# An attention and highway kernel: the first quad loaded and squared in halves, and the whole order planned again

## The chip, the cores and the metric

The kernel runs on one core of a Trainium2 chip. The metric is the device time of one execution in microseconds. Thirteen runs of the kernel before have a median of 274.4 us and lie between 272.18 and 276.83 us.

The core has five engines that run their own instruction lists in order. TensorE (PE) multiplies matrices and transposes. VectorE (DVE), ScalarE (ACT) and GpSimd (POOL) work on tiles, and SyncE (SP) issues most of the transfers. [...]

## The reference

```python
# q, k, v: (8, 12, 448, 64) float32; tau = 0.1
q_n = q / (norm(q, axis=-1) + 1e-6)
k_n = k / (norm(k, axis=-1) + 1e-6)
scores = q_n @ k_n.T / tau
attn = softmax(scores, axis=-1)
x = (attn @ v)                  # heads side by side: (3584, 768)
H = relu(x @ w_h)
T = sigmoid(x @ w_t + b_t)      # w_h, w_t: (768, 768)
out = T * H + (1 - T) * x
```

Because q_n and k_n have unit length, the scores are bounded, and the kernel takes no maximum before the exponential.

## The kernel before

**Tiles.** A *quad* is four heads of one batch, so there are 24 quads, three for each of eight batches. The q part (t = 0) and the k part (t = 1) of a quad have each 4 x 448 rows of 64 elements. They are held as 128 partitions by 14 groups by 64 elements, in one `raw` tile in float32: two halves of 7 groups, 448 elements in each partition.

**Steps of a quad.**

- `load_qk` (L279) issues one transfer of 448 KB for q and one for k on SyncE. The k load of quad 0 is issued on ScalarE's queue instead (L288). `load_v` (L301) does the same for v.
- `squares` (L353) makes `sq`, in float16, on ScalarE (one operation of 896 elements), on VectorE, or on GpSimd (two of 448). VectorE sums each group of 64 into `n2` (L392), and for some quads GpSimd first adds the two half rows (`folds`, L409).
- `rsqrt_act` (L436) makes the inverse norm `rs` with two ScalarE operations, Ln and Exp, over q and k together. Later quads use Newton steps on VectorE in `rsqrt` (L451).
- `norms` (L512) multiplies `raw` by `rs` into `qn`, on VectorE (one operation for each of q and k) or on GpSimd (two). `qn` is then transposed into `qT`, either by seven TensorE transposes and a copy, or by a DMA transpose on SyncE.
- `cast_v` (L578) casts v to float16 into `vm`, on ScalarE or VectorE.
- `quad` (L603) computes seven sets of scores on TensorE (L624) into `sp` in PSUM, two buffers of it. ScalarE takes their exponential into `e` (L635), 896 elements an operation, 168 in all. TensorE multiplies `e` with `vm` into `u` (L675), and VectorE divides by the sum into `x` (L726). From quad 12 on, two sets of scores go out together.

**The feed-forward part.** `ffn` (L757) and `quarters` (L796) take 28 row tiles of `x`, transpose them to `xT`, and multiply them with the two weights in matmuls of 384 columns (L818). Tanh on ScalarE gives the gate. VectorE, or for some tiles GpSimd, combines the result (L836 to L911). The weights come by four transfers that GpSimd issues (`load_w`, L323). The first row tile can start only when the first batch's attention is done, so its work runs some quads behind the attention and alone at the end.

**What sets the order.** Each step is registered as an operation with an engine, an assumed duration, a due time and what it depends on. `Plan.run` (L55) then goes through all of them once, before the program is built. It keeps a clock for each engine, picks the ready operation with the smallest start plus a share of its due time, and so fixes the order in which every engine gets its instructions. On the chip these orders are fixed; only the waits move. Which engine does a step is written out in strings, one letter for each quad or row tile (L221 to L235): `SQ_E` for squares, `NORM` for norms, `TURN` for transposes and their copies, `VM` for the casts of v, `XT` for the transposes of x, `GATE` and `BIAS` for the feed-forward part.

For transfers the planner keeps one shared clock `dma_free`. It lets SyncE issue when that clock is at most 5 us ahead, and it takes a load as done 1.1 us after its data (L148). A matmul group whose tile shape differs from that of the one before it is charged 93 ns (`SWITCH`). The shapes are "quad" (scores), "row" (`u`) and "full" (the rest).

Of the kernel before, what the change touches and what calls it, by code (L numbers as in the profile page):

```python
# [8 lines left out]
FP32 = mybir.dt.float32  # L9
FP16 = mybir.dt.float16  # L10
# [10 lines left out]
class Plan:  # L21
# [7 lines left out]
    AHEAD = 15  # L29
    NEAR = 60  # L30
    LATE = 0.04

    def __init__(self):
        self.ops = []
# [20 lines left out]
    def run(self):  # L55
        for o in self.ops:
# [7 lines left out]
                    after.update((x.n, x) for x in d[1][:1] if x is not o)  # L64
            o.after = [x for n, x in after.items() if n not in deps]
            o.deps = list(deps.values())
        t_eng = {e: 0 for e in self.LAT}
        left = {o.n: len(o.deps) + len(o.after) for o in self.ops}
        outs = {o.n: [] for o in self.ops}
        for o in self.ops:  # L70
# [5 lines left out]
        while back:  # L76
            o = back.pop()
            due = 1e9 if o.pri is None else o.pri[0] if isinstance(o.pri, tuple) else o.pri
            for c in outs[o.n] if not isinstance(o.pri, tuple) else ():
                lat = o.dur + self.LAT[o.eng] + (o.size + 2000 if o.size else 0)  # L80
                due = min(due, c.pri - (self.SLACK * lat / 1000 if o in c.deps else 0))
            o.pri = due
            for d in o.deps + o.after:
                users[d.n] -= 1
                if not users[d.n]:
                    back.append(d)

        def arm(o):
            r = 0
# [16 lines left out]
        mode = ""  # L106
# [3 lines left out]
        while len(order) < len(self.ops):  # L110
            best = None
            for e, L in ready.items():
                if not L:
                    continue
                t = t_eng[e]
                pick = None
                for r, o in L:
                    s = max(t, r)
                    if e == "DVE" and o.kind == "lock":
                        s = max(s, port[0])  # L120
                    elif e == "POOL":
                        s = max(s, port[1])
                    elif e == "SP" and len(lanes) >= 8:
                        s = max(s, lanes[-8])
                    if e == "SP":
                        s = max(s, dma_free - 5000)
                    k = (max(s, t + self.NEAR) + (e != "SP") * self.LATE * 1000 * o.pri, o.pri, o.n)
                    if pick is None or k < pick[0]:
                        pick = (k, s, r, o)
                if best is None or pick[1] < best[1]:  # L130
                    best = pick
            _, s, r, o = best
            e = o.eng
            ready[e].remove((r, o))
            end = s + o.dur
            if e == "PE":
                if o.kind != mode:
                    end += self.SWITCH
                mode = o.kind
            elif e == "POOL":  # L140
                port[0] = end
            elif e == "DVE" and o.kind == "lock":
                port[1] = end
            t_eng[e] = end
            o.start, o.done = s, end
            if o.size:
                dma_free = max(dma_free, end + (-700 if o.kind == "turn" else 900)) + o.size
                o.done = dma_free + 1100  # L148
            if e == "SP":
                lanes.append(o.done)  # L150
            order.append(o)
            for c in outs[o.n]:
                left[c.n] -= 1
                if not left[c.n]:
                    arm(c)
# [7 lines left out]
def kernel(  # L163
# [18 lines left out]
    C = 7  # L182
# [35 lines left out]
    ones_row = const.tile([128, 128], FP16)  # L218
    eps = const.tile([128, 1], FP32)
    NV = 2  # L220
    SQ_E = ("APAAAAAAPAAAAAPAPAPAAAAP", "PPAPPPPPAAAAAAAAAAPPPAAA")  # L221
    FOLDS = "000000010102012120000110"
    NORM = ("DDDPPPPPPPPPPPPPPPPPDPPP", "DPPPPPPPPPPPPPPPPPPPPDPP")
    TURN = ("ADDDSSSSSSSSSSSSSSSSSSSS", "DDDDASSSSSSSSSSSSSSSSSSS")
    XT = "DDDDDDDDAAAAADSSASSSSSSSSSSS"
    ENG = {"A": "ACT", "D": "DVE", "P": "POOL"}
    PAIR = 12
    LEAD = 4
    GATE = "RRRRRRRRRDRRRRRPRRDRPPPRPRRD"
    BIAS = "MMMMMMMMMMMMMMMDDDMMDDDDDDDM"  # L230
    LATER = 3
    W_AT = 16
    RS = "AAAAAAADDDDDDDDDDDDDDDDD"
    SW_AT = 52
    VM = "UAAUAAUUDUUDDUDDUDDUUUUU"  # L235
    TAIL = 6
    vm_b = [const.tile([128, 6, C, 66], FP16, name=f"vm{i}") for i in range(NV)]
    e_b = [const.tile([128, 14 * S + 64], FP16, name=f"e{i}") for i in range(2)]
# [34 lines left out]

    o_fb = op("DVE", 700, -1, [], fill_b)


    raw_ops, sq_ops = {}, {}

    def load_qk(Q):  # L279
        b, qd = divmod(Q, NQ)  # L280
        ring, wait = P.buf("raw", N_RAW)
        st["ring_raw", Q] = ring
        got = []
        for t in range(2):
            def f(t=t):
                if t == 0:
                    st["raw", Q] = raw_p.tile([128, NG, D], FP32, name="raw")
                eng = nc.scalar if Q == 0 and t else nc.sync  # L288
                eng.dma_start(
                    st["raw", Q][:, NT * t : NT * t + NT].rearrange("x (h c) d -> x h (c d)", h=2),  # L290
                    (q, k)[t][b, 4 * qd : 4 * qd + 4]
                    .rearrange("n (p c) d -> (n p) (c d)", c=C)
                    .rearrange("(h x) f -> x h f", x=128),
                )
            o = op("SP", 60 if Q == 0 and t else 550, None, wait, f, kind="load", size=1200)
            wait = [("first", [o])] + wait if not got else wait
            got.append(o)
            ring.append(o)
        st["got", Q] = got

    def load_v(b):  # L301
# [51 lines left out]
    def squares(Q):  # L353
# [5 lines left out]
        for t in range(2):  # L359
# [4 lines left out]
            def f(t=t, eng=eng):  # L364
# [6 lines left out]
                else:  # L371
                    nc.gpsimd.tensor_mul(o[:, 0:C, :], i[:, 0:C, :], i[:, 0:C, :])  # L372

            def f2(t=t):
                o, i = st["sq", Q, t][:, C:NT, :], st["raw", Q][:, NT * t + C : NT * t + NT, :]
                nc.gpsimd.tensor_mul(o, i, i)  # L376

            a = op(eng, {"ACT": 840, "DVE": 1000, "POOL": 900}[eng], None,
                   wait + st["got", Q][t : t + 1], f, kind="lock" if eng == "DVE" else "")
            both = [a, a]  # L380
            if eng == "POOL":
                both[1] = op(eng, 900, None, [("first", [a])] + st["got", Q][t : t + 1], f2)
            ring += both
            st["ring_raw", Q] += both
            if not level:
# [46 lines left out]
        return [last]  # L432

    logs, switch = [], []

    def rsqrt_act(b, qd, reds):  # L436

        def f():
            n2, rs = nrm_tiles(b)
            nc.scalar.activation(rs[:, qd, :], n2[:, qd, :], AF.Ln, bias=eps[:, :])  # L440

        def g():
            rs = nrm_tiles(b)[1]
            nc.scalar.activation(rs[:, qd, :], rs[:, qd, :], AF.Exp, scale=-0.5)

        a = op("ACT", 200, None, reds + [o_fb, o_fe], f)
        z = op("ACT", 120, None, [a], g)
        logs.append(z)
        return z

    def rsqrt(b, qd, n, reds):  # L451
        due = None
# [52 lines left out]
        for it in range(2):  # L505
            for i in range(3 if eng == "DVE" else 4):
                last = op(eng, lens[0] if eng == "DVE" else lens[1], due, [last], newton(i, it),
                          kind="lock" if eng == "DVE" else "")
                ring_ta.append(last)
        return last  # L510

    def norms(Q, rs_op):  # L512
        b, qd = divmod(Q, NQ)
        for t in range(2):
            ring, wait = P.buf(f"qn{t}", N_QN)
            eng = ENG[NORM[t][Q]]

            parts = [(0, 2, 0, C)] if eng == "DVE" else [
                (h, h + 1, c0, c1) for h in range(2) for c0, c1 in ((0, C),)
            ]  # L520
            done = []
            for h0, h1, c0, c1 in parts:
                def f(t=t, eng=eng, h0=h0, h1=h1, c0=c0, c1=c1):
                    if h0 == 0 and c0 == 0:
                        st["qn", Q, t] = qn_p.tile([128, C, 128], FP16, name=f"qn{t}")
                    g = slice(NT * t, NT * t + NT)
                    rs = nrm_tiles(b)[1]
                    (nc.vector if eng == "DVE" else nc.gpsimd).tensor_mul(  # L528
                        st["qn", Q, t][:, :, :].rearrange("p c (h d) -> p h c d", h=2)[:, h0:h1, c0:c1, :],
                        st["raw", Q][:, g, :].rearrange("p (h c) d -> p h c d", h=2)[:, h0:h1, c0:c1, :],  # L530
                        rs[:, qd, g].rearrange("p (h c) -> p h c", h=2)[:, h0:h1, c0:c1]
                        .unsqueeze(3).to_broadcast([128, h1 - h0, c1 - c0, D]),
                    )

                n = (h1 - h0) * (c1 - c0) * D
                done.append(op(
                    eng, 1000 if eng == "DVE" else 145 + 1.68 * n, None,
                    ([("first", done[:1])] if done else wait) + [rs_op] + st["got", Q], f,
                    kind="lock" if eng == "DVE" else "",
                ))  # L540
            ring += done
            st["ring_raw", Q] += done
            st["ring_n", b] += done
# [2 lines left out]
            if TURN[t][Q] != "S":  # L546
                ringp, waitp = P.buf("pt", 2)

                def g(t=t):
                    st["tp", Q, t] = p_ps.tile([128, C, 128], FP16, name="tp", tag="pt")  # L550
                    for c in range(C):
                        nc.tensor.transpose(  # L552
                            st["tp", Q, t][:, c, :], st["qn", Q, t][:, c, :], ident[:, :]
                        )
# [3 lines left out]
                    copy = nc.scalar.copy if TURN[t][Q] == "A" else nc.vector.tensor_copy  # L558
                    copy(st["qT", Q, t][:, :, :], st["tp", Q, t][:, :, :])

                w = op("PE", 360, None, done + [o_id] + waitp, g, kind="full")
                z = op(ENG[TURN[t][Q]], 840 if TURN[t][Q] == "A" else 540, None, [w] + wait2, h)
                ringp += [w, z]
                ring += [w]
            else:
                def g(t=t):
                    st["qT", Q, t] = qt_p.tile([128, C, 128], FP16, name=f"qT{t}")
# [10 lines left out]
    def cast_v(b):  # L578
# [3 lines left out]
        for i in range(NQ):  # L582
            how = VM[NQ * b + i]
            got = []
            for h0, n in ((0, 1), (1, 1)) if how == "U" else ((0, 2),):
                def f(g=slice(2 * i + h0, 2 * i + h0 + n), how=how):
# [2 lines left out]
                        st["vr", b][:, g, :].rearrange("p i (c d) -> p i c d", c=C),  # L589
                    )  # L590
                got.append(op(
                    "ACT" if how == "A" else "DVE", {"A": 840, "D": 540, "U": 530}[how], None,
                    wait + [o_fv[b % NV], st["gotv", b][i]], f, kind="lock" if how == "D" else "",
                ))
            outs.append(got)
# [432 lines left out]
```

## Time and profile before

The page gives one profiled execution. Its own time was 274.4 us, and the span from its first to its last instruction is 272.6 us.

| Engine | busy us | share of the span | instructions |
|---|---|---|---|
| PE, matmuls | 240.3 | 88% | 4221 |
| PEld, weight loads beside them | 137.2 | 50% | 4221 |
| DVE | 226.1 | 83% | 496 |
| ACT | 207.7 | 76% | 284 |
| POOL | 154.7 | 57% | 170 |

| Group | count | mean ns | idle before it |
|---|---|---|---|
| ACT exponentials `e`<-`sp`, L635 | 168 | 922 | 19.7 us, of it 19.3 waiting for scores |
| PE feed-forward `pt`<-`w`,`xT`, L818 | 600 | 327 | 3.9 us |
| PE `u`<-`vm`,`e`, L675 | 2688 | 195 | 6.3 us |
| PE scores `sp`<-`qT`,`qT`, L624 | 672 | 377 | 3.8 us |
| POOL norms `qn`<-`raw`,`rs`, L528 | 84 | 970 | 42.5 us |
| ACT squares `sq`<-`raw`, L368 | 32 | 968 | 4.8 us, of it 4.5 waiting for loads of q |

A group's row gives the operation's duration and the idle time of its engine just before it, with what ended that idle time. The duration of a matmul includes its way through the array, so many overlap, and 600 x 327 ns are not 600 turns of the engine. An engine's share of the whole span hides that the kernel passes through stages: at the start little runs, in the middle attention and feed-forward overlap, and in the last 30 us only feed-forward is left. Windows of the trace show these stages apart.

### The profile page before, as it was taken

How to read it: one execution, taken by the hardware profiler on the slowest of the kernel's cores; microseconds unless marked ns; L12 is line 12 of the kernel's file. 1: busy time of each engine (PE TensorE's matmuls, PEld its weight loads, DVE VectorE, ACT ScalarE, POOL GpSimd, SP SyncE). 2: the span in 40 equal slices, each digit the busy share in tenths (PEclk: the TensorE clock that was granted, in tenths of full speed). 3: DMA queues.
4: the chain of work that ended last, by engine and by line, in shares of the span. 5: the costliest groups of instructions: out<-in, count | busy, mean ns of one | idle time of the engine just before them, and what ended most of it. 6: DMA issues, size and time to landing. Idle time of an engine off the chain costs nothing. (4 is left out here: it accounts for less than half of the span.)

```text
span 272.6 us, 9928 instructions
## 1 busy us (share of the span) xinstructions
PE 240.3 (88%) x4221; PEld 137.2 (50%) x4221; DVE 226.1 (83%) x496; ACT 207.7 (76%) x284; POOL 154.7 (57%) x170
## 2 busy tenths in 40 slices
PE   0277869989699999999999999999899999998991
PEld 0235546545345456555655556455456455565560
DVE  2998578499889989887999999899998786579793
ACT  3498799998979897899888898997677687821220
POOL 2869487975284993599419943976085004460500
PEclk9999798999999999999999999999999999999999
DMA  7999969998989999999999899999758535315323
GB/s 250 381 386 328 232 127 303 172 272 257 320 201 304 152 255 217 327 190 262 315 350 199 247 261 239 206 248 266 203 119 142 134 82 90 89 58 142 109 101 115
DMA packets 72061, 58.95 MB, mean 216 GB/s; under 512 B 48336, under 2 KB 68304, under 8 KB 72016
## 3 DMA queue, kind: packets, MB, share of 16 engines
q1 hardware_dynamic: 70144, 55.49, 79.7%
q0 software_dynamic: 1600, 2.36, 4.8%
q8 instruction: 33, 0.54, 0.8%
q10 hardware_dynamic: 272, 0.46, 0.5%
q14 instruction: 12, 0.10, 0.1%
HBM read 38.14 MB, written 11.01 MB: 180 GB/s over the span
## 5 line engine op out<-in xcount | busy, mean ns | idle before, releaser
L635 ACT ACTIVATE e<-sp 128x896 f16<-128x896 f32 x168 | 145.8, 922 | 19.7 <-PE sp L624 19.3
L818 PE MATMUL pt<-w,xT 128*128 128x384 f16 x600 | 116.2, 327 | 3.9 <-DVE o L911 1.7
L528 POOL TENSOR_TENSOR qn<-raw,rs 128x448 f16<-128x448 f32 x84 | 78.9, 970 | 42.5 <-DVE rs L494 36.3
L818 PEld LDWEIGHTS <-xT 128*128 128x128 f16 x672 | 59.2, 98 | 52.1 <-issue 16.1
L675 PE MATMUL u<-vm,e 64*128 64x65 f16 x2688 | 59.1, 195 | 6.3 <-DVE x L726 2.5
L675 PEld LDWEIGHTS <-e 64*128 64x128 f16 x2688 | 49.2, 97 | 30.3 <-issue 19.6
L624 PE MATMUL sp<-qT,qT 64*64 64x448 f16 x672 | 55.8, 377 | 3.8 <-ACT e L635 2.5
L392 DVE TENSOR_REDUCE n<-sq 128x7 f32<-128x448 f16 x60 | 34.3, 608 | 6.2 <-ACT sq L368 6.2
L889 DVE SCALAR_TENSOR_TENSOR pt<-tt,pt 128x384 f32<-128x384 f16 x56 | 31.3, 560 | 8.7 <-ACT tt L846 4.9
L368 ACT ACTIVATE sq<-raw 128x896 f16<-128x896 f32 x32 | 30.2, 968 | 4.8 <-DMA raw<-in_q_dram 4.5
L624 PEld LDWEIGHTS <-qT 64*64 64x64 f16 x672 | 15.6, 105 | 27.6 <-issue 22.5
L846 ACT ACTIVATE tt<-pt 128x384 f16<-128x384 f32 x44 | 21.9, 498 | 9.5 <-DVE pt L836 5.6
L726 DVE TENSOR_TENSOR x<-u,rd 128x384 f16<-128x384 f32 x48 | 24.5, 551 | 0.7
L904 DVE SCALAR_TENSOR_TENSOR pt<-pt,x 128x384 f32<-128x384 f32 x36 | 20.2, 561 | 5.7 <-PE pt L818 3.7
L419 POOL TENSOR_TENSOR fold<-sq 128x448 f32<-128x448 f16 x18 | 18.7, 1056 | 9.3 <-ACT sq L368 9.3
L372 POOL TENSOR_TENSOR sq<-raw 128x448 f16<-128x448 f32 x16 | 16.2, 1010 | 12.2 <-DMA raw<-in_k_dram 6.6
L846 ACT ACTIVATE tt<-sp 128x384 f16<-128x384 f32 x12 | 5.9, 490 | 21.1 <-DVE sp L836 19.2
L587 DVE CAST vm<-vr 128x448 f16<-128x448 f32 (+1 forms) x33 | 21.4, 669 | 0.1
L911 DVE SCALAR_TENSOR_TENSOR o<-x,pt 128x384 f32<-128x384 f16 x36 | 19.8, 550 | 0.7
L552 PE MATMUL tp<-ident,qn 128*128 128x128 f16 x63 | 6.7, 270 | 12.0 <-DVE qn L528 12.0
L857 POOL TENSOR_TENSOR g<-tt,x 128x384 f16<-128x384 f16 x8 | 7.3, 912 | 16.4 <-ACT tt L846 16.4
L376 POOL TENSOR_TENSOR sq<-raw 128x448 f16<-128x448 f32 x16 | 16.0, 1002 | 0.0
(53 smaller groups left out, 174.4 us busy)
## 6 DMA issues: line engine op xcount, KB each, us to landing
raw<-in_q_dram SPq DMA_DIRECT2D x24, 448.0 KB, 6.4
vr<-in_v_dram SPq DMA_DIRECT2D x24, 448.0 KB, 5.1
raw<-in_k_dram SPq DMA_DIRECT2D x23, 448.0 KB, 6.5
out_dram<-o SPq DMA_DIRECT2D x24, 384.0 KB, 3.5
out_dram<-o SPq DMA_DIRECT2D x8, 192.0 KB, 2.9
w<-in_moe_w_t_dram POOLq DMA_DIRECT2D x2, 576.0 KB, 11.7
w<-in_moe_w_h_dram POOLq DMA_DIRECT2D x2, 576.0 KB, 13.0
qT<-qn SPq DMA_TRANSPOSE x39, 4.1
```

What stands on the lines that cost most here:

```text
L368: nc.scalar.activation(o, i, AF.Square)
L392: nc.vector.reduce_sum(n2[:, qd, NT * t + g0 : NT * t + g0 + n], src()[:, g0 : g0 + n, 0:width], axis=AX.X,)
L528: (nc.vector if eng == "DVE" else nc.gpsimd).tensor_mul(st["qn", Q, t][:, :, :].rearrange("p c (h d) -> p h c d", h=2)[:, h0:h1, c0:c1, :] ...
L587: (nc.scalar.copy if how == "A" else nc.vector.tensor_copy)(vm[:, g, :, 0:D], st["vr", b][:, g, :].rearrange("p i (c d) -> p i c d", c=C),)
L624: nc.tensor.matmul(sp[64 * half : 64 * half + 64, h, 0:S].rearrange("x (c p) -> x c p", c=C), lhsT=kT[hp, ci, 64 * half : 64 * half + 64], ...
L635: nc.scalar.activation(e[:, o : o + 2 * S].rearrange("x (a p c) -> x a p c", a=2, c=C), st["sp", Q, ci][:, :, 0:S].rearrange("x a (c p) -> ...
L675: nc.tensor.matmul(u[:, s, slot * (D + 1) : (slot + 1) * (D + 1)], lhsT=e[sp, o : o + 128], rhs=vm[sp, 2 * qd + h, c, 0 : D + 1], start=(c ...
L726: nc.vector.tensor_mul(st["x", b][:, :, 4 * qd : 4 * qd + 4, :].rearrange("p t (h s) d -> p t h s d", s=2)[:, :, :, s, :], u[:, s, :, 0:D] ...
L818: nc.tensor.matmul(loc["pt", qi], lhsT=loc["xT"][:, cc, :] if cc < CC else ones_row[:, :], rhs=w_f[w_i][:, cc, ms] if cc < CC else bth[:, ms],
L846: nc.scalar.activation(loc["tt", mh][:, :], loc["pt", qi], AF.Tanh)
L889: nc.vector.scalar_tensor_tensor(out=h, in0=loc["tt", mh][:, :], scalar=1.0, in1=h, op0=ALU.add, op1=ALU.mult)
L904: nc.vector.scalar_tensor_tensor(out=h, in0=h, scalar=0.0, in1=xf()[:, ms], op0=ALU.max, op1=ALU.subtract)
```

## The change

Quad 0 is loaded in four transfers of 224 KB (q first half, q second half, k first half, k second half), all on SyncE. Both its squares are made on ScalarE, in halves that each wait for their own transfer. Its Ln and Exp are split into one pair for q and one for k, and the Exp writes into a PSUM tile `u`, from which the norms of quad 0 read. These norms run on VectorE in two pieces each (4 and 3 groups), and the transposes follow in pieces of 4 and 3.

The planner's rules are changed: loads are taken as done 1.7 us after their data and held until the transfer clock is at most 3 us ahead; all engines start at 0.7 us; and on TensorE an operation whose shape differs from the last one is charged 60 ns more in the choice. The letters that give steps to engines are other ones, and with them and the new rules the order of the whole kernel is another. Two hooks, `NUDGE` and `WARM`, are added and do nothing with the values given.

```diff
@@ class Plan
+    MODE = 60
+    QUEUE = 3000
...
-        t_eng = {e: 0 for e in self.LAT}
+        t_eng = {e: 700 for e in self.LAT}
...
-                        s = max(s, dma_free - 5000)
-                    k = (max(s, t + self.NEAR) + (e != "SP") * self.LATE * 1000 * o.pri, o.pri, o.n)
+                        s = max(s, dma_free - (self.QUEUE if o.kind == "load" else 5000))
+                    k = (max(s, t + self.NEAR) + (e != "SP") * self.LATE * 1000 * o.pri
+                         + (e == "PE" and o.kind != mode) * self.MODE, o.pri, o.n)
...
-                o.done = dma_free + 1100
+                o.done = dma_free + (1700 if o.kind == "load" else 1100)
@@ the letters
-    SQ_E = ("APAAAAAAPAAAAAPAPAPAAAAP", "PPAPPPPPAAAAAAAAAAPPPAAA")
-    FOLDS = "000000010102012120000110"
-    NORM = ("DDDPPPPPPPPPPPPPPPPPDPPP", "DPPPPPPPPPPPPPPPPPPPPDPP")
-    TURN = ("ADDDSSSSSSSSSSSSSSSSSSSS", "DDDDASSSSSSSSSSSSSSSSSSS")
-    XT = "DDDDDDDDAAAAADSSASSSSSSSSSSS"
+    SQ_E = ("AAAADPAAPAAAAAPAAPPAPPAP", "APPPPPPDAAAAAAAAAADAAAAA")
+    FOLDS = "000000002102012212101110"
+    NORM = ("DDDDDPPPPPPDDPPPPPPPPPDD", "DPPPPPPPPPPPPPPPPPPPPPPP")
+    TURN = ("DDDAADSSSDSSSSSSSSSSSSSS", "ADDDDSSDDSSSSSSSSSSSSSSS")
+    XT = "DDDADASDSSADDSSSSSASSSSSSSSS"
...
-    GATE = "RRRRRRRRRDRRRRRPRRDRPPPRPRRD"
-    BIAS = "MMMMMMMMMMMMMMMDDDMMDDDDDDDM"
+    GATE = "RRRRRRRRRRRRRRRPRRDRPPPRRRRD"
+    BIAS = "MMMMMMMMMMMMMDMDDDMMDDDDDDDM"
-    W_AT = 16
+    W_AT = 20
+    SPLIT = "100000000000000000000000"
-    SW_AT = 52
-    VM = "UAAUAAUUDUUDDUDDUDDUUUUU"
+    SW_AT = 40
+    VM = "DAAAAAUUAUDUUUDUUUAAAAAA"
@@ load_qk
-        for t in range(2):
+        for t, h, n in ((0, 0, 1), (0, 1, 1), (1, 0, 1), (1, 1, 1)) if Q == 0 else ((0, 0, 2), (1, 0, 2)):
...
-                eng = nc.scalar if Q == 0 and t else nc.sync
-                eng.dma_start(
+                hs = slice(2 * h, 2 * h + 2 * n)
+                nc.sync.dma_start(
@@ squares
+                a = op(eng, 460, None, wait + got[:1], lambda fq=fq: fq(0))
+                both = [a, op(eng, 460, None, [("first", [a])] + got[1:], lambda fq=fq: fq(1))]
@@ rsqrt_act, for each of the two parts of quad 0
+                nc.scalar.activation(rs[:, qd, gs], n2[:, qd, gs], AF.Ln, bias=eps[:, :])
...
+                    if part[0] == 0:
+                        st["rsp"] = u_ps.tile([128, 2, 512], FP32, name="u")
+                    o = st["rsp"][:, part[0], 0:NT]
+                nc.scalar.activation(o, rs[:, qd, gs], AF.Exp, scale=-0.5)
@@ norms
-            parts = [(0, 2, 0, C)] if eng == "DVE" else [
+            parts = [(0, 2, 0, C)] if eng == "DVE" and Q else [
+                (0, 2, 0, 4), (0, 2, 4, C)
+            ] if eng == "DVE" else [
...
+                    of = rs[:, qd, g] if Q else st["rsp"][:, t, 0:NT]
...
-                    ([("first", done[:1])] if done else wait) + [rs_op] + st["got", Q], f,
-                    kind="lock" if eng == "DVE" else "",
+                    ([("first", done[:1])] if done else wait) + [rs_op[t]] + st["got", Q][t], f,
+                    kind="lock" if eng == "DVE" and Q else "",
...
+                    ws = [op("PE", 220, None, done[:1] + [o_id] + waitp, lambda g=g: g(range(4)), kind="full")]
+                    ws.append(op("PE", 160, None, done[1:] + [("first", ws[:1])], lambda g=g: g(range(4, C)), kind="full"))
```

## The prediction

> **What bounds the kernel now.** I first read the windows of 10 us (columns: the stretch and its length; busy us and count on PE, PEld, DVE, ACT, POOL; granted clock; DMA share; GB/s).
>
> ```profile
> 30.00:40.00 10.00, 7.03 (x176) 4.89 (x177) 5.26 (x13) 9.11 (x15) 6.99 (x8) 0.84 0.91 166
> 60.00:70.00 10.00, 8.48 (x184) 4.60 (x183) 9.53 (x25) 8.72 (x11) 5.09 (x6) 1.00 0.91 277
> 110.00:120.00 10.00, 10.00 (x198) 5.46 (x198) 8.54 (x20) 9.20 (x12) 7.69 (x9) 1.00 1.07 288
> 160.00:170.00 10.00, 10.00 (x231) 5.91 (x230) 9.44 (x26) 9.18 (x13) 2.73 (x3) 1.00 1.03 252
> 210.00:220.00 10.00, 10.00 (x178) 5.30 (x172) 7.91 (x17) 7.59 (x11) 0.00 (x0) 1.00 0.59 151
> ```
>
> See that up to about 75 us ScalarE is the fullest engine while TensorE has gaps; later TensorE has none, with VectorE and ScalarE near 90% behind it. The chain of waits agrees: from 202 to 240 us it names only TensorE.
>
> ```profile
> 209.38 0.50 PE sp L624 x8
> 209.88 0.55 PE u L675 x28
> 210.43 1.73 PE pt L818 x10
> ```
>
> Busy time is not price on this engine, since a matmul's row holds its latency (326 ns mean at L818). So I read start to start in TensorE's timeline.
>
> ```profile
> 99.59 0.66 PE L818 MATMUL pt<-w,xT 128*128 128x384 f16 x3
> 100.18 0.38 PE L624 MATMUL sp<-qT,qT 64*64 64x448 f16 x4
> 100.49 1.15 PE L818 MATMUL pt<-w,xT 128*128 128x384 f16 x6
> 101.48 0.33 PE L818 MATMUL pt<-bth,ones_row 128*128 128x384 f16 x1
> 101.73 0.57 PE L624 MATMUL sp<-qT,qT 64*64 64x448 f16 x8
> 102.24 0.51 PE L774 MATMUL xp<-ident,xtail 128*128 128x128 f16 x6
> ```
>
> Three pt take 0.59 us and seven take 1.24, so one costs 0.163 and the group 0.10 on top. Four sp take 0.31 and eight 0.51: 0.05 each, 0.11 on top. Groups of u (28 in 0.55, 56 in 0.99) give 0.0157 each and 0.11. **Every change of tile shape costs TensorE about 0.11 us**, and the order of before has 280 of them: 31 us of a saturated engine.
>
> Last, the head, in the timeline of all engines.
>
> ```profile
> 5.20 0.95 ACT L368 ACTIVATE sq<-raw 128x896 f16<-128x896 f32 x1 [3.18 <-DMA raw<-in_q_dram]
> 5.54 0.93 POOL L372 TENSOR_TENSOR sq<-raw 128x448 f16<-128x448 f32 x1 [4.23 <-DMA raw<-in_k_dram]
> 8.41 0.32 ACT L440 ACTIVATE rs<-n,eps 128x28 f32<-128x28 f32 x1 [2.26 <-DVE n L392]
> 9.02 2.83 DVE L528 TENSOR_TENSOR qn<-raw,rs 128x896 f16<-128x896 f32 x2
> 12.87 0.62 DVE L559 COPY qT<-tp 128x896 f16<-128x896 f16 x1 [0.50 <-PE tp L552]
> 13.55 0.96 PE L624 MATMUL sp<-qT,qT 64*64 64x448 f16 x8 [0.72 <-DVE qT L559]
> 14.19 1.73 ACT L635 ACTIVATE e<-sp 128x896 f16<-128x896 f32 x2 [1.29 <-PE sp L624]
> ```
>
> Nothing covers this chain: load, square, sum, norm, transpose, copy. ScalarE's 168 exponentials start only at 14.19.
>
> **The head.** Four half loads leave on SyncE at 0.49 us each (its row of before), so the last is issued near 2.2 us instead of 0.77 on ScalarE's queue. [...] If the 1.5 us of extra issue were all paid, the last half would land at 5.54 + 1.5 = 7.0. The slice row shows 381 GB/s here, so a half of 224 KB takes 0.59 us, longer than its issue: the halves follow one another behind the same data. I take the row: the first lands about 3.6 us, the last about 5.3. ScalarE then squares four halves. [...] In the trace exponentials of 896 follow every 0.868 us and tanh of 384 every 0.38: 0.96 ns an element and almost nothing fixed, so a half costs 0.44 and splitting 0.06. [...] Last square done at 5.9, its sum at 6.5. GpSimd's 1.8 us for k (5.54 to 7.36) leaves the chain. Ln and Exp are split too, q's running during k's sums. The four norm pieces have 512 or 384 elements: the nearest row, x<-u,rd from PSUM, has 384 in 0.47 us start to start, so 0.6 + 0.47, twice: 2.1 against 2.83, since the pair of before ran into a GpSimd square (1.69 for the second, 1.14 for the first; that square took 1.80). Norms end at 8.7, transposes at 9.1, ScalarE's copy (0.89) at 10.1, first exponential 10.8: **3.4 us earlier**. The bounds are 0 (the next quad decides) and 3.9. Quad 1 keeps GpSimd squares and its k load arrives no earlier, but its Ln waited behind exponentials and sums (15.80), not on the load; I pass on 3.2.
>
> **TensorE by order.** Counted in the two built programs' instruction orders, which hold no time: changes of shape go from 280 to 235, minus 45 x 0.11 = -4.9 us. Transposes of qn go from 63 to 98, those of x from 90 to 72: +17 x 0.057 (six in 0.34) = +1.0. Two bias matmuls fewer: -0.3. Net -4.2. By groups of four quads (112 matmul sets of scores): 0, +2.7, -2.5, -2.9, -0.2, 0, and -1.1 after the last scores; the +2.7 is feed-forward and transposes moved earlier.
>
> **ScalarE.** Casts of v 4 to 12: +8 x 0.83; one qT copy more +0.8, one xT copy fewer -0.7, one square fewer -0.85, one Ln more +0.2: +6.1 us. In orders: quads 4 to 7 get +2.8 (37.3 to 40.1 us of ScalarE work in a stretch that lasted 39.5: it sticks out, I charge +1.0); quads 16 to 19 +2.2 (33.5 in 38.5, hidden under TensorE); quads 20 to 23 +2.8 (35.5 in a stretch of 35.5; charged +1.0, nothing if the casts fall in ScalarE's waits for scores, the full 2.8 if not). Stretch lengths come from the exponentials' busy time in the windows, 0.868 us each. These casts were hidden before on VectorE.
>
> **VectorE** sheds 12 casts (-8.4), 12 sums of 448 but gains 6 of folds (-4), gains four full norms (+6), four qT copies less two xT (+1.4), 2 us of feed-forward operations, and three squares that the trace of before lacks. Nearest is the norm of 896, 1.09 to 1.89 us by GpSimd's interference; I take 1.3, +3.9 in all, 3.3 to 5.7 at the ends. Together about +1, but moved forward: +6 in quads 0 to 3, where it had 7 us idle between 30 and 50 us; -2 to -4 in quads 8 to 11 and 16 to 23. GpSimd loses about 6 us and is at 57%: nothing. Gates: one late feed-forward tile leaves GpSimd's pair (0.92 + 0.91), on the chain at 253.12 to 255.03, for VectorE: up to -0.7, inside the tail's -1.1.
>
> **Queues.** Five qT transposes leave SyncE, three xT come. Loads are held until 3 us of data is queued rather than 5, and count as done 0.6 us later. Trace: loads took 6.4 us to land and, after the head, no wait on raw is large; later issue could cost a load's wait of 1 us or gain as much on transposes behind it; I take 0.
>
> **Sum.** Head -3.2; quads 4 to 7 +1.0; quads 8 to 11 limited next by VectorE's 34.8, so -1.3 of 2.5; quads 12 to 15 -2.7; 16 to 19 -0.2; 20 to 23 +1.0; tail -1.1: -6.5. Each engine is then above 90% in order, and waits grow; before, a stretch lasted 0.5 to 2.5 us above its largest sum. I keep -5.0. The span of 272.6 becomes 267.6. The profiled execution's time was 274.4, 1.8 more, and equals the median of the runs: **269.4 us**, chance 0.47.
>
> **Rivals.** (a) *Everything lands:* the stages give up -6.5 and the two charges are hidden: 274.4 - 8 = 266.4. For: ScalarE has 28.8 us idle between first and last exponential. Against: three engines near their sums. 0.14.
> (b) *The weights come late.* Their start time goes from 16 to 20 us, the last issue behind quad 3's norm near 31 instead of 25.9; they took 10.8 to 13.1 us to land, so 44. Feed-forward starts half a quad earlier in order: 45.8 - 3.2 - 2 = 40.6. TensorE would stand 3 us in a stretch where ScalarE waits behind it: 272.5. Against: VectorE and ScalarE may delay its start anyway. 0.13.
> (c) *Hidden:* the next quads' loads or VectorE (9.5 of 10 busy at 10 to 20 us) take the head, TensorE's saved switches turn into waits: 273.8. 0.12.
> (d) *ScalarE becomes the bound, and it is slower.* Place: exponentials from quad 4 on. If the 28.8 us of waits stay, because paired scores still come late in larger groups (two score buffers), the added 6.1 us are paid in full, and larger groups (my estimate) add 0.5 us of such waits in each of four stretches: 274.4 - 3.2 + 6.1 + 2.0 - 1.1 for the tail = 278.2. It decides once ScalarE's waits on scores stay above 17 us (19.3 now). Against: those waits were TensorE's own fullness, which falls. 0.14.
>
> **Numbers.** 0.5% is 1.4 us, about what this kernel's runs can tell from nothing. Faster (below 273.0): all of the forecast and (a), 0.08 of (b), 0.03 of (c): 0.72. Same: the rest of (b) and (c), with 0.01 of (d): 0.15. Slower: 0.13. The range of 266.0 to 275.0 leaves out most of (d) and a low edge of (a).
>
> **What would show it.** Right: first exponential near 10.8; 235 shape changes at the same 0.11; last exponential's end near 234 instead of 239.5; the tail after it about 1 us shorter; no TensorE gap at the first pt. Wrong: a wait of the first pt on w; ScalarE above 95% in quads 4 to 7 or waits on scores above 20 us; a wait of VectorE or ScalarE on raw past 20 us; score groups after which TensorE idles.

## The result and the profile after

The changed kernel takes 267.88 us (median of 11 runs, 267.30 to 269.53). The kernel before, run beside it, takes 274.25 (48 runs, 271.34 to 276.83). The ratio is 0.981, with a 95% interval from 0.977 to 0.984: about 6 us faster, with 269.4 forecast and 266.0 to 275.0 as the range. The profiled execution of after took 268.86 us, 1 us above the median, and its span is 267.1 where before's was 272.6. Ratios, here and below, leave out runs that were disturbed, and so can differ a little from the quotient of two medians. (The diff above misprints the new `XT`. It is "DDDADASADSSADDSSSSSASSSSSSSS", and the counts of the prediction were made with that.)

These are the same five windows of after as were read of before, in the same columns (stretch, length, busy us and count on PE, PEld, DVE, ACT and POOL, granted clock, DMA share, GB/s).

```profile
30.00:40.00 10.00, 7.47 (x182) 5.22 (x175) 7.05 (x14) 9.97 (x16) 8.66 (x9) 0.83 1.12 266
60.00:70.00 10.00, 9.77 (x228) 5.93 (x228) 9.47 (x27) 9.85 (x14) 6.68 (x8) 1.00 1.04 260
110.00:120.00 10.00, 10.00 (x216) 5.74 (x209) 9.08 (x20) 9.38 (x13) 9.92 (x11) 1.00 0.90 184
160.00:170.00 10.00, 10.00 (x206) 5.58 (x202) 9.51 (x27) 9.26 (x12) 2.94 (x4) 1.00 1.08 280
210.00:220.00 10.00, 10.00 (x223) 5.93 (x219) 5.73 (x13) 8.51 (x12) 0.07 (x1) 1.00 0.80 130
```

ScalarE is full at 60 to 70 us (9.85 of 10, before 8.72), and TensorE's gaps there have gone (9.77, before 8.48). At 210 to 220 VectorE is down from 7.91 to 5.73: the late casts of v have left it. The groups of exponentials and scores in after, and the scores in before:

```profile
L703 ACT ACTIVATE e<-sp 128x896 f16<-128x896 f32 x168 | 145.5, 925 | 11.1 <-PE sp L692 10.6
L692 PE MATMUL sp<-qT,qT 64*64 64x448 f16 x672 | 53.9, 376 | 8.1 <-ACT e L703 7.0
L624 PE MATMUL sp<-qT,qT 64*64 64x448 f16 x672 | 55.8, 377 | 3.8 <-ACT e L635 2.5
```

ScalarE waits 10.6 us for scores, where it waited 19.3, and TensorE now waits 7.0 us for ScalarE to empty a score buffer, where it waited 2.5. The time saved on TensorE has turned in part into waits on the next engine.

The price of a change of tile shape is read again in TensorE's timeline of after.

```profile
230.11 2.11 PE L886 MATMUL pt<-w,xT 128*128 128x384 f16 x12
232.15 0.57 PE L692 MATMUL sp<-qT,qT 64*64 64x448 f16 x8
232.65 0.84 PE L743 MATMUL u<-vm,e 64*128 64x65 f16 x42
233.42 0.66 PE L886 MATMUL pt<-w,xT 128*128 128x384 f16 x3
```

Start to start, 12 pt take 2.04 us (12 x 0.163 + 0.10 = 2.06), 8 sp take 0.50 and 42 u take 0.77 (42 x 0.0157 + 0.11 = 0.77). The prices of before hold in after.

Then the head, in the timeline of all engines.

```profile
0.74 0.87 SPq L312 DMA_DIRECT2D raw<-in_q_dram  x2
1.66 0.91 SPq L312 DMA_DIRECT2D raw<-in_k_dram  x2
3.31 1.23 ACT L405 ACTIVATE sq<-raw 128x448 f16<-128x448 f32 x2 [1.29 <-DMA raw<-in_q_dram]
5.70 0.58 ACT L405 ACTIVATE sq<-raw 128x448 f16<-128x448 f32 x1 [1.17 <-DMA raw<-in_k_dram]
7.43 0.58 ACT L405 ACTIVATE sq<-raw 128x448 f16<-128x448 f32 x1 [1.16 <-DMA raw<-in_k_dram]
9.57 1.61 DVE L588 TENSOR_TENSOR qn<-raw,u 128x384 f16<-128x384 f32 x3 [0.32 <-ACT u L497]
13.44 1.71 ACT L703 ACTIVATE e<-sp 128x896 f16<-128x896 f32 x2
```

The q halves are squared early, but ScalarE stands idle before each k half, and the last one can be squared only at 7.43. The first exponential comes at 13.44, which is 0.75 us earlier than before and not 3.4. What the DMA engines moved from 3 to 5 us, while these loads were in flight, is the last figure (GB/s) of these windows of before, after and e4. The last is a kernel described below, which loads the first quad whole again.

```profile
3.00:5.00 2.00, 0.00 (x0) 0.00 (x0) 0.00 (x0) 0.00 (x0) 0.00 (x0) 1.00 1.05 381
3.00:5.00 2.00, 0.00 (x0) 0.00 (x0) 1.05 (x2) 1.15 (x2) 0.00 (x0) 1.00 0.88 266
3.00:5.00 2.00, 0.00 (x0) 0.00 (x0) 0.00 (x0) 0.00 (x0) 0.00 (x0) 1.00 1.04 393
```

At the start of the feed-forward part TensorE's timeline shows the wait that rival (b) named.

```profile
44.55 0.65 PE L886 MATMUL pt<-w,xT 128*128 128x384 f16 x3
47.13 0.65 PE L886 MATMUL pt<-w,xT 128*128 128x384 f16 x3 [1.93 <-DMA w<-in_moe_w_h_dram]
47.70 0.57 PE L692 MATMUL sp<-qT,qT 64*64 64x448 f16 x8
```

How the difference builds up is read from the first exponential of each quad, after against before. The stages are differences of these; "quads 20 to 23" ends with the last exponential, and the last row is what follows it.

| stage | forecast us | measured us | standing at its end |
|---|---|---|---|
| head | -3.2 | -0.75 | -0.75 |
| quads 0 to 3 | 0 | -1.22 | -1.97 |
| quads 4 to 7 | +1.0 | -1.12 | -3.09 |
| quads 8 to 11 | -1.3 | -0.50 | -3.59 |
| quads 12 to 15 | -2.7 | +0.20 | -3.39 |
| quads 16 to 19 | -0.2 | -1.52 | -4.91 |
| quads 20 to 23 | +1.0 | -0.32 | -5.23 |
| after the last exponential | -1.1 | -0.27 | -5.5 |

The sums agree, -6.5 with -5.0 kept and -5.5 measured. The stages don't. So the experiments ask which parts of the change pay.

Each column of times is from one execution, and some of the experiments show how far that carries. e7, e10 and e12 below have the same instruction order as after on every engine up to 176 us. Their heads measure -0.53 to -1.18, and quads 8 to 11 -0.87 to -1.23; the other stages up to quad 15 agree with the table within 0.1. e6 has the order of before up to 188 us and yet stands 1.4 to 1.5 us later from quad 7 to quad 18. So a single stage is good to about 1 us, and quads 4 to 7 may have gained more than 1.12.

### The profile page after: what moved, and what is told of

Same layout as the page of the kernel before. It is cut to its first block, busy times and chain, and to the rows that moved or that the text cites. A ratio compares the mean times of both kernels' runs of the same rounds, so it can differ in the third digit from the quotient of the medians.

```text
span 267.1 us, 9962 instructions
## 1 busy us (share of the span) xinstructions
PE 236.1 (88%) x4236; PEld 136.4 (51%) x4236; DVE 223.8 (84%) x493; ACT 213.3 (80%) x295; POOL 148.2 (56%) x164
## 4 chain that ended last, share of the span: by engine, by line
PE 54%; DVE 21%; DMA 11%; ACT 7%; issue 3%; SPq 1%; DVEq 0%; ACTq 0%
PE pt L886 26%; PE u L743 12%; PE sp L692 11%; DMA w<-in_moe_w_h_dram 6%; ACT e L703 5%; DVE pt L957 4%; DVE pt L972 3%; DVE o L979 3%; DMA vr<-in_v_dram 3%; DVE n L432 2%; DVE x L794 2%; DMA raw<-in_k_dram 2%; PE sp L886 2%; PE xp L842 2%; PE tp L616 2%
## 5 line engine op out<-in xcount | busy, mean ns | idle before, releaser
L703 ACT ACTIVATE e<-sp 128x896 f16<-128x896 f32 x168 | 145.5, 925 | 11.1 <-PE sp L692 10.6
L588 POOL TENSOR_TENSOR qn<-raw,rs 128x448 f16<-128x448 f32 x76 | 74.0, 1004 | 39.1 <-DVE rs L551 19.4
L743 PE MATMUL u<-vm,e 64*128 64x65 f16 x2688 | 54.5, 192 | 0.6 <-issue 0.6
L459 POOL TENSOR_TENSOR fold<-sq 128x448 f32<-128x448 f16 x24 | 24.7, 1039 | 14.9 <-ACT sq L395 13.5
L432 DVE TENSOR_REDUCE n<-sq 128x7 f32<-128x448 f16 x48 | 27.7, 608 | 5.0 <-ACT sq L405 4.1
L395 ACT ACTIVATE sq<-raw 128x896 f16<-128x896 f32 x29 | 27.7, 965 | 0.0
L616 PE MATMUL tp<-ident,qn 128*128 128x128 f16 x98 | 9.9, 258 | 10.4 <-DVE qn L588 9.6
L399 POOL TENSOR_TENSOR sq<-raw 128x448 f16<-128x448 f32 x14 | 13.1, 934 | 10.8 <-DMA raw<-in_k_dram 8.9
L886 PE MATMUL sp<-w,xT 128*128 128x384 f16 x72 | 13.7, 326 | 1.7 <-DMA xT<-x 1.7
L616 PEld LDWEIGHTS <-qn 128*128 128x128 f16 x98 | 7.3, 116 | 13.5 <-DVE qn L588 10.6
L776 DVE RECIPROCAL rd<-u 128x12 f32<-128x12 f32 (+1 forms) x48 | 9.7, 202 | 5.0 <-PE u L743 4.5
```

Of the source, the lines that this page charges most:

```text
L395: nc.scalar.activation(o, i, AF.Square)
L432: nc.vector.reduce_sum(n2[:, qd, NT * t + g0 : NT * t + g0 + n], src()[:, g0 : g0 + n, 0:width], axis=AX.X,)
L588: (nc.vector if eng == "DVE" else nc.gpsimd).tensor_mul(st["qn", Q, t][:, :, :].rearrange("p c (h d) -> p h c d", h=2)[:, h0:h1, c0:c1, :] ...
L703: nc.scalar.activation(e[:, o : o + 2 * S].rearrange("x (a p c) -> x a p c", a=2, c=C), st["sp", Q, ci][:, :, 0:S].rearrange("x a (c p) -> ...
L743: nc.tensor.matmul(u[:, s, slot * (D + 1) : (slot + 1) * (D + 1)], lhsT=e[sp, o : o + 128], rhs=vm[sp, 2 * qd + h, c, 0 : D + 1], start=(c ...
L886: nc.tensor.matmul(loc["pt", qi], lhsT=loc["xT"][:, cc, :] if cc < CC else ones_row[:, :], rhs=w_f[w_i][:, cc, ms] if cc < CC else bth[:, ms],
```

## The experiments

Medians of kernels that ran together stand beside the same runs of before: 274.25 for e1 to e4, 274.15 for e5 to e8, 273.99 for e9 to e12. Times inside a kernel come from one profiled execution of it.

**e1: the head alone.** The kernel before with `load_qk`, `squares`, `rsqrt_act` and `norms` of after; rules and letters stay, but for the square of k in quad 0. (The planner's assumed durations of squares, norms and casts are those of after in e1 and e8.)

```diff
-    SQ_E = ("APAAAAAAPAAAAAPAPAPAAAAP", "PPAPPPPPAAAAAAAAAAPPPAAA")
+    SQ_E = ("APAAAAAAPAAAAAPAPAPAAAAP", "APAPPPPPAAAAAAAAAAPPPAAA")
```

> The kernel before with the new head alone (half loads, half squares, inverse norms in PSUM; old planner rules, old letters but ScalarE for the k squares of quad 0); 278 changes of tile shape on TensorE against 280. If the head carries the gain as sized in the prediction (3.2 us): 271. If it carries only what the trace of the changed kernel shows at the first exponential (0.75 us): 273.5. If what matters is the number of shape changes or the letters: 273.5 to 274.5, since neither moves.

Measured 274.91, ratio 0.9995 [0.995, 1.004]. The first exponential started at 12.47 us, 1.7 earlier, and the last one ended at 235.75, 3.8 earlier; the tail behind it grew from 33.06 to 34.85 us in the profile. That execution was the fastest of e1's twelve (272.40), and by their median the runs gained nothing. The head alone, with this order of the tail, is worth no time that can be measured.

**e2: the grouping of shapes alone.**

```diff
-                    k = (max(s, t + self.NEAR) + (e != "SP") * self.LATE * 1000 * o.pri, o.pri, o.n)
+                    k = (max(s, t + self.NEAR) + (e != "SP") * self.LATE * 1000 * o.pri
+                         + (e == "PE" and o.kind != mode) * 60, o.pri, o.n)
```

> The kernel before with one thing more in the planner's choice: 60 ns against a change of tile shape on TensorE. 239 changes against 280, all letters and the head as before. If shape changes are the price of the middle (0.11 us each, some 35 of the 41 in the stretch where TensorE has no gap): about 270.3. If the letters or the head carry the gain: 274 within 1.

Measured 274.19, ratio 1.0005 [0.997, 1.004], with 239 changes of shape instead of 280. By quad 13 the exponentials were 4.97 us ahead of before. At quad 23 1.70 was left, and the tail was 1.6 us longer.

**e3: after without the grouping.**

```diff
-    MODE = 60
+    MODE = 0
```

> The changed kernel with that 60 ns set to 0: 265 changes against 235. Shape changes: 267.9 + 30 x 0.11 = 271.2, somewhat less where TensorE has gaps. Letters or head: 268 within 1.

Measured 272.62, ratio 0.998 [0.994, 1.002], with 265 changes of shape: 4.7 us above after. The same rule that brought nothing in e2 is worth most of the gain here.

**e4: after with the first quad loaded whole,** k on ScalarE's queue as before; squares, norms and all else as in after.

```diff
-        for t, h, n in ((0, 0, 1), (0, 1, 1), (1, 0, 1), (1, 1, 1)) if Q == 0 else ((0, 0, 2), (1, 0, 2)):
+        for t, h, n in ((0, 0, 2), (1, 0, 2)):
...
-                nc.sync.dma_start(
+                (nc.scalar if Q == 0 and t else nc.sync).dma_start(
```

> The changed kernel with quad 0 loaded as before: two whole transfers, k issued on ScalarE's queue; squares still in halves, inverse norms still in PSUM; 238 shape changes against 235. If half loads gain what the prediction gave them: first exponential 2 us or more later and 270 or above. If the loads are bound by the data and not by how they are cut: first exponential within 0.7 us of 13.44 either way, and 267.3 to 268.6. If halves on one queue cost (the last k half landed at 7.4 us, the whole k of before at 5.5): first exponential earlier, 12 to 13, and up to 1 us faster.

Measured 267.00 (266.43 to 267.86), ratio 0.976 [0.9714, 0.9805]: 0.9 us below after. Its head, in ScalarE's timeline:

```profile
5.15 1.97 ACT L405 ACTIVATE sq<-raw 128x448 f16<-128x448 f32 x4 [3.13 <-DMA raw<-in_q_dram]
7.03 0.29 ACT L488 ACTIVATE rs<-n,eps 128x14 f32<-128x14 f32 x1
```

Two whole transfers of 448 KB on two queues let all four squares run from 5.15 us without a pause, so the last begins at 6.56, and the first exponential starts at 12.73. In the seven profiles with this head in halves (after, e1, e3, e7, e8, e10, e12) the last square began between 5.9 and 7.7 us, 6.9 in the middle of them. So loading in halves gained nothing, and the kernel with whole loads is a little faster. How much of the 0.9 us is the loads' own isn't shown: with after's letters the first exponential lies between 12.80 and 13.66 with halves (after, e3, e7, e10, e12) and at 12.73 and 12.80 with wholes (e4, e11), and the order of all that follows is another too.

**e5: grouping and late casts; e6: late casts alone.** Both are the kernel before with six of the last casts of v on ScalarE; e5 has the rule of e2 too.

```diff
-    VM = "UAAUAAUUDUUDDUDDUDDUUUUU"
+    VM = "UAAUAAUUDUUDDUDDUDAAAAAA"
```

> The kernel before with 60 ns against a change of tile shape (239 changes, as in e2) and its six latest casts of v, which were on VectorE, on ScalarE. Theory 'two engines in turn' (TensorE is full to about 180 us, VectorE from 180 to 220, so fewer shape changes pay only if VectorE is relieved there): 271 to 272. Theory 'number of shape changes has no price by itself, the letters as a whole do': 274.

> The kernel before with the six latest casts of v on ScalarE and nothing else (284 shape changes). Two engines in turn: TensorE keeps its full stretch to 180 us, so no more than 1 us: 273 to 274.5. If late VectorE work alone set the end: 271.

e5: 274.67 (271.41 to 279.83), ratio 0.9954 [0.9905, 1.0003], no gain that can be told from nothing. e6: 275.31, ratio 1.001 [0.997, 1.006]. With these orders the casts don't make the grouping pay. (e5's tail is 36.2 us, with the same wait as in e7 below, so a gain ahead of it could be lost there too.)

**e7: after with the late casts back on VectorE; e8: after's head and rules with the letters of before.**

```diff
@@ e7
-    VM = "DAAAAAUUAUDUUUDUUUAAAAAA"
+    VM = "DAAAAAUUAUDUUUDUUUUUUUUU"
@@ e8: SQ_E, FOLDS, NORM, TURN, XT, GATE, BIAS, W_AT, SW_AT and VM, the first of them
-    SQ_E = ("AAAADPAAPAAAAAPAAPPAPPAP", "APPPPPPDAAAAAAAAAADAAAAA")
+    SQ_E = ("APAAAAAAPAAAAAPAPAPAAAAP", "APAPPPPPAAAAAAAAAAPPPAAA")
...
```

> The changed kernel with the six latest casts of v back on VectorE (237 shape changes against 235). Two engines in turn: VectorE gets 3.5 us more between 180 and 225 us, and 1.5 to 3 of it shows: 269.5 to 271. If ScalarE was the engine to spare late (it waits 10 us on scores) or VectorE has room: 267 to 268.5.

> The changed kernel with the letters of before (engines of squares, norms, turns, casts, gates; W_AT and SW_AT too), but ScalarE for quad 0's k squares: so the new head and the new planner rules alone, 238 shape changes. If the letters are what lets the grouping pay: 273 to 275, as e1 and e2. If head, grouping and load rules together carry it: 270 or below.

e7: 271.87, ratio 0.992 [0.988, 0.996], 4.0 us above after. e8: 275.74, ratio 1.006 [1.002, 1.010], 7.9 above after and slower than before. In e7 the last exponential ends at 234.85, half a microsecond from after's 234.31. All the rest is lost behind it, which TensorE's timeline of e7 shows:

```profile
232.68 0.57 PE L692 MATMUL sp<-qT,qT 64*64 64x448 f16 x8
233.22 1.62 PE L886 MATMUL pt<-w,xT 128*128 128x384 f16 x9
234.68 1.14 PE L886 MATMUL sp<-w,xT 128*128 128x384 f16 x6
235.65 0.65 PE L886 MATMUL pt<-w,xT 128*128 128x384 f16 x3
236.14 1.14 PE L886 MATMUL sp<-w,xT 128*128 128x384 f16 x6
237.11 1.14 PE L886 MATMUL pt<-w,xT 128*128 128x384 f16 x6
238.09 0.65 PE L886 MATMUL sp<-w,xT 128*128 128x384 f16 x3
238.67 0.62 PE L743 MATMUL u<-vm,e 64*128 64x65 f16 x28
239.22 0.66 PE L886 MATMUL sp<-w,xT 128*128 128x384 f16 x3
239.82 1.14 PE L886 MATMUL pt<-w,xT 128*128 128x384 f16 x6
240.79 0.65 PE L886 MATMUL sp<-w,xT 128*128 128x384 f16 x3
241.37 1.51 PE L743 MATMUL u<-vm,e 64*128 64x65 f16 x84
242.82 0.66 PE L886 MATMUL sp<-w,xT 128*128 128x384 f16 x3
243.32 1.14 PE L886 MATMUL pt<-w,xT 128*128 128x384 f16 x6
244.61 0.62 PE L743 MATMUL u<-vm,e 64*128 64x65 f16 x28 [0.15 <-DVE x L794]
247.50 1.88 PE L886 MATMUL sp<-w,xT 128*128 128x384 f16 x6 [2.27 <-DMA xT<-x]
249.17 2.13 PE L886 MATMUL pt<-w,xT 128*128 128x384 f16 x6
251.09 1.18 PE L886 MATMUL sp<-w,xT 128*128 128x384 f16 x6
```

Between the last scores (232.68) and the last quad's attention output (u x84 at 241.37, its last 28 at 244.61) PE's order has 45 feed-forward matmuls: 33 ahead of the first u and 12 behind it. (The expectation of e10 below says 39, a miscount.) When all that is done, the last row tiles still have to be divided, transposed by DMA and brought back, and TensorE stands 2.27 us with the rest of its matmuls waiting for them. Then the same six matmuls take 2.13 us instead of 1.14: the clock has fallen, to a mean of 0.54 over the 3.4 us from 247.50 us on. This execution of e7 took 273.15 us, 1.3 above e7's median, so not every run need have that stretch. That gave a new theory. **The order of the tail decides what an earlier attention is worth.** The planner's order puts 36 such matmuls there in before, 42 in e2, and 27 in after and e4.

**e9 to e12: the last quad's output first.** In four kernels the attention output of the last quad gets due times 10 us earlier through the `NUDGE` hook (added to the kernel before in e9). Numbers of changes of shape stay as they were, and so does the order of every engine up to some 234 us.

```diff
+            if Q == NQUAD - 1 or (Q == NQUAD - 2 and rnd):
+                last_ops.extend(ops)
...
+    P.NUDGE = {o.n: -10 for o in last_ops}
```

> The kernel before with the grouping of matmul shapes alone (as e2), and the attention output of the last quad (its u matmuls, reciprocals and x products) given due times 10 us earlier, so that PE's order has 12 feed-forward matmuls between the last scores and the last quad's attention output instead of 42; shape changes and everything else as in e2. Theory of the order in the tail (what the grouping gains ahead of the last exponential was given back because the last quad's output came late in PE's order): from the last exponential's end to the first matmul on the last batch's transposed x about 10.6 us instead of 12.7, the wait on that transpose below 1.7 us, no half-clock stretch behind it, time about 272.2. Rival (the feed-forward matmuls that are put behind take the same time there, and the tail is bound by VectorE's adds and norms): no change, 274.2, last exponential near 238 and a tail of 34.6 us as in e2.

> The kernel after with the letters of e7 (the late casts back on VectorE), and the last quad's attention output given due times 10 us earlier: 12 feed-forward matmuls ahead of it instead of 39. Theory of the order in the tail: the letters cost 4.0 us in e7 through the order that they led to and not through VectorE, so that about 3 of these come back: time about 269.0, last exponential near 234.9 as in e7, tail about 33 us instead of 36.5, granted clock near 1 behind the wait on the transpose. Rival (VectorE, 19.06 of 20 us busy at 190 to 210 us in e7 against 16.94, is what costs): no change, 271.9.

> The kernel of e4 (after, with the first quad loaded whole on two queues) and the last quad's attention output given due times 10 us earlier: 15 feed-forward matmuls ahead of it instead of 27. Theory of the order in the tail: a little of the wait on the last transpose goes, 265.5 to 266.5 against e4's 267.0. Rival: no change, 267.0.

> The kernel after with the last quad's attention output given due times 10 us earlier and nothing else changed: 15 feed-forward matmuls ahead of it instead of 27. Theory of the order in the tail: up to 1 us shorter, about 267.0 against 267.9, and e11 stays about 0.9 below it (the cost of the half loads). Rival (the matmuls put behind take their time later): 267.9, and the difference to e11 stays.

The first, third and fifth column are of one profiled execution each, "matmuls" is PE's order, "wait" TensorE's on the last transpose of x, "tail" what follows the last exponential.

| kernel | last exponential ends | matmuls ahead of the last output | wait us | tail us | median us | ratio to before |
|---|---|---|---|---|---|---|
| e2 | 237.97 | 42 | 2.30 | 34.63 | 274.19 | 1.0005 |
| e9, its order mended | 236.37 | 12 | none | 32.93 | 271.34 | 0.993 [0.9893, 0.9965] |
| e7 | 234.85 | 45 | 2.27 | 36.55 | 271.87 | 0.992 |
| e10, its order mended | 233.81 | 12 | none | 32.69 | 268.98 | 0.981 [0.976, 0.986] |
| e4 | 233.62 | 27 | 1.59 | 32.48 | 267.00 | 0.976 |
| e11, its order mended | 232.54 | 15 | none | 31.86 | 266.55 | 0.973 [0.968, 0.978] |
| after | 234.31 | 27 | 1.66 | 32.79 | 267.88 | 0.981 |
| e12, its order mended | 233.15 | 15 | none | 32.05 | 267.57 | 0.976 [0.971, 0.981] |

TensorE's timeline of e10:

```profile
231.64 0.57 PE L692 MATMUL sp<-qT,qT 64*64 64x448 f16 x8
...
234.91 1.51 PE L743 MATMUL u<-vm,e 64*128 64x65 f16 x84
...
238.41 0.62 PE L743 MATMUL u<-vm,e 64*128 64x65 f16 x28
238.97 1.15 PE L892 MATMUL pt<-w,xT 128*128 128x384 f16 x6
239.95 1.14 PE L892 MATMUL sp<-w,xT 128*128 128x384 f16 x6
240.93 1.14 PE L892 MATMUL pt<-w,xT 128*128 128x384 f16 x6
```

The last output now comes 3.3 us after the last scores instead of 8.7. The matmuls that were ahead of it cover its way through VectorE and the DMA, and nothing waits. The theory is borne out where it foretold most, in e9 and e10 (2.9 us each by the medians, 2.1 and 3.0 by the ratios, with about 2 and 3 expected), and the rivals, that the matmuls only take their time later and that VectorE is what costs in e7, fall. In e11 and e12, where the wait had been 1.6 us, 0.5 and 0.3 us came by the medians and 0.9 and 1.3 by the ratios, which isn't clear of the noise. In all four the last exponential also ends 1.0 to 1.6 us earlier in the profile. The edit can't have done that, since the orders are the same up to there; it is the difference between one execution and another. What the profiles show of the edit is the shorter tail: 1.7, 3.9, 0.6 and 0.7 us for e9 to e12. Whole loads stay about 1 us ahead of halves with this order too (266.55 against 267.57). **e11 is the fastest kernel here,** 1.3 us below after.

The step from e7 to e10 can be followed in the profiles. The tail shrank by 36.55 - 32.69 = 3.86 us. Of it 2.27 was the wait, and a stretch of 3.4 us at a granted clock of 0.54 cost, as an estimate, 0.46 x 3.4 = 1.6. By the medians 2.9 us came, since e7's profile was one of its slower executions and e10's its fastest.

## Why the prediction was right, point by point

- **The head: the step that failed.** "The last about 5.3" was 7.43 in the profile of after: 2.1 of the 2.6 us that are missing between the 10.8 of the forecast and 13.44. The norms and what follows them took some 0.5 us more. In three more executions with the same order of the head (e7, e10, e12) the last square began at 6.9 to 7.7 us. What went wrong is the rate: the forecast took 381 GB/s, at which whole loads move, for halves. (Its 381 is the slice from 6.8 us on, but before has the same from 3 to 5 us.) From 3 to 5 us the seven profiles with whole loads (before, e2, e4, e5, e6, e9, e11) have 379 to 410 GB/s, and the seven with halves 255 to 284. Other loads, issued from 2.61 us on, moved in that time too: by 7 us after had moved 1.46 MB (209 GB/s over 7 us), and the four halves are 0.92. The bound of 7.0 was nearer, with 6.9 in the middle of seven profiles.
- **The squares in halves, and what the head is worth:** four half squares in e4 take 1.97 us with 0.58 for one, so (1.97 - 0.58) / 3 = 0.46 from start to start. The forecast's 0.44, an estimate from the turns of exponentials and tanh in the trace of before, was near it. But e1 shows a second fault: even 1.7 us of head brought the runs nothing by itself, so that passing on all but 0.2 us of it was unfounded. (In e1's profile the last exponential was 3.8 us earlier, and the tail took 1.8 of that back.)
- **Changes of shape:** 235, and each still 0.10 to 0.11 us. But 45 x 0.11 is not what they bring. In e2 41 fewer brought no time. In e3 30 more than after (3.3 us by the price) moved the last exponential by 1.8 us and lengthened the tail by 1.3. What they need beside them is the order of the tail, for which e9 speaks (by itself the grouping brought nothing, and with the last output early 2.7 us against before), and the letters; how the letters help ahead of the last exponential is not shown. The forecast counted letters and grouping as separate terms, and e3 and e8 show that the gain needs both.
- **ScalarE:** forecast +6.1 us of work, measured 207.7 to 213.3, +5.6. The two charges of 1.0 were too dear. In quads 4 to 7 the stretch became 1.1 us shorter, although the window at 60 to 70 is full. In quads 20 to 23 the casts pay: e10 and e12 differ only by them and the order that follows, and e12, with the casts on ScalarE, is 1.4 us faster. ScalarE's waits for scores hide them, at least in part: from 195 us on these are 4.4 us in e10 and 2.1 in e12. Rival (d) fell by its own sign: these waits went to 10.6 us, and 17 was its bound.
- **VectorE:** about +1 forecast; its busy time went from 226.1 to 223.8. The three new squares took 1.07, 1.60 and 1.36 us, 1.345 in the mean, with 1.3 taken.
- **The weights, rival (b):** they came late, and later than rival (b) had them, in use at 47.13 and not 44. TensorE stood 1.93 us and not 3, since the first pt was late too, at 43.40 instead of 40.6. The exponentials of quads 5 and 6 are back at before's times (-0.12 and +0.42 us) and at quad 7 2.53 ahead again. The same wait is 0.27 us in e4 and 1.87 in e11, which have the same order up to there and stand 1.5 and 1.6 us ahead of before at quad 5, so it was taken up.
- **Queues:** 0 was right as far as seen; loads of q and k took 6.4 to 6.5 us to land in before and 6.4 in after. Loads of v went from 5.1 to 6.9, and past 20 us the profile puts one wait down to them, 2.3 us of GpSimd.
- **The tail:** -1.1 forecast, -0.27 measured. The forecast counted matmuls and not what they wait for: the wait on the last transpose grew from 0.74 to 1.66 us.
- **The sum:** the last exponential's end was foretold near 234 and is 234.31, the span 267.6 and is 267.1. That it agrees is partly luck, and the runs' 267.88 lie as near to rival (a)'s 266.4 as to the 269.4. The stages give 7.0 us too much (2.5 for the head, 2.9 in quads 12 to 15, 0.8 each in quads 8 to 11 and in the tail) and 6.0 too little (quads 0 to 7 and 16 to 23), and the reserve of 1.5 us more than covers the 1.0 between them. Two slips in the working stand beside this sum: from 60 to 70 us VectorE (9.53 us) was fuller than ScalarE (8.72), and rival (a)'s 6.5 and 2.0 make 8.5 and not 8.

**What stays open.** Which of the letters help ahead of the last exponential wasn't taken apart. e1, e3 and e8 also have 42 to 45 matmuls ahead of the last output and waits of 2.2 us; they weren't run with their order mended, so how much of the 4.7 and 7.9 us is the tail's is known only from single profiles (1.3 and 3.2 us). Nor was before run with the mended order alone, so e9's gain is the two edits together. (Before waits only 0.74 us on its last transpose, so less should be had there than in e11 and e12; that is argued and not run.)

## What to carry to other kernels

A saving in the middle of a kernel reaches the end only if the last stage can start on what comes early: before you price a part, look at what the in-order engine has been given between the last result of one stage and the first operation that sends it on to the next. Price parts of a planned order together as well as alone, since grouping and the letters each brought nothing without the other. And a transfer split so that work can begin earlier has to be judged by when its last piece lands.

## What the runs showed of the hardware

**The clock fell after a wait of 2.3 us.** In six profiles (e1, e2, e3, e5, e7, e8) TensorE waited 2.2 to 2.3 us for the last transpose. In three of them (e5, e7, e8) the clock granted then was about half for some 3.4 us: in windows of 1 us it was 0.63, 0.50, 0.50 and 0.66 in e7, then 1.00. Two windows of e7 behind its wait:

```profile
247.50:250.90 3.40, 3.40 (x12) 1.70 (x13) 0.56 (x1) 0.49 (x1) 0.00 (x0) 0.54 0.87 214
251.00:254.00 3.00, 3.00 (x19) 1.80 (x18) 2.53 (x5) 0.49 (x1) 0.00 (x0) 0.97 0.00 0
```

The clock is the third number from the end. It is 0.54 with 12 matmuls in 3.4 us, then 0.97 with 19 in 3. In the tails of before, after and e4, with waits of 0.74 to 1.66 us, it didn't fall in this way: it was 1.00 in every window of 2 us from 232 to 264 us. In e1, e2 and e3, with waits as long as in the three, it was 1.00 in each of the 6 us behind the wait. So such a wait doesn't always bring a fall, and what decides is not shown.

**Halves moved slower and landed later than wholes.** Four transfers of 224 KB on one queue were all issued by 2.6 us, and the last was in use between 5.9 and 7.7 us (seven profiles). Two of 448 KB on two queues were in use at 5.20 and 5.54 us in before; in e4 q was at 5.15 and k by 6.10. From 3 to 5 us the DMA engines moved 255 to 284 GB/s with halves and 379 to 410 with wholes (seven profiles each). Size and queue were changed together. Against the queue as the cause speaks that in before whole loads from SyncE alone moved 378 to 393 GB/s in each us from 7 to 12; halves on two queues weren't run.
